# The last phase of an attention and two-layer kernel: element-wise stages of different later steps in one fixed order on each engine, and finished sums copied out by two engines

## The chip, the cores and the metric

The kernel runs on one core of a Trainium2 chip. The core has five engines that work side by side: PE (TensorE, matrix products), DVE (VectorE), ACT (ScalarE), POOL (GpSimd) and SP (SyncE, which here only issues transfers). The metric is the device time of one launch in microseconds (us); lower is better. Before the change it is 1274.14 us (median of three runs, 1273.32 to 1274.87).

## The reference, cut to what matters

```python
# q, k, v: (4, 12, 448, 64);  x between the parts: (1792, 768);  w_in: (768, 2048), w_out: (2048, 768)
q_n, k_n = rmsnorm(q, g_q), rmsnorm(k, g_k)
attn = softmax(q_n @ k_n.T / sqrt(64))
x = (attn @ v), heads put side by side      # 1792 tokens x 768
h = x @ w_in;  g = s * relu(h)**2 + b;  x = g @ w_out      # first layer
h = x @ w_in2; g = h * cos(h);          x = g @ w_out2     # second layer
```

All is float32. The change lies in the second layer: nearly all of it in its last line's second half, `g = h * cos(h)` and `g @ w_out2`.

## The kernel before, in words

Every float32 operand of a product is split in a high part (rounded to the matrix engine's float32 form) and a low part, `hi + lo`, and a product is the sum of three: hi·hi, lo·hi, hi·lo. So each operand costs a cast (ACT) and a subtraction (POOL or DVE).

The second layer has two phases. **Phase one** makes `h` in eight chunks of 256 of the 2048 columns, for two halves `pr` of the tokens (896 tokens each, "0" and "1"). From chunk 2 on for half 0, and from chunk 3 on for half 1, a chunk of one half is seven products of combined operands in place of eight (Strassen's scheme): the combined tokens are the tiles `x_t` (`t1` to `t4`, each in three pieces c), the combined weights `ps`. `mix_tasks` makes the `t` tiles in 21 small tasks; `chunk_tasks` hands such tasks to the steps of the chunk ahead, and `spread_out` spaces each list evenly over that chunk's steps. `h` goes to DRAM (`hd`).

**Phase two** (`second_out`) makes the output. The 14 blocks of 128 tokens are taken in five groups of 3, 3, 3, 3 and 2 (`GROUPS`). A group is 16 steps, one for each 128 of the 2048 rows of `w_out2`; a step multiplies the group's piece of `g` (the tile `gp`: hi and lo) with that weight (`wo_h`, `wo_l`): 18 matmuls with three blocks, 12 with two, into one PSUM bank for each block and half of the output columns. A group of three holds six of the eight banks. When its sixteenth step is done DVE copies each bank out (`o`, line 1209), and SP stores it. The next group has two banks that are free; for the third it needs the first copy.

For every step, piece by piece: SP fetches `h` (`ask`, five steps ahead, tile `g`); then `prepare_g`, three steps ahead, runs the whole chain for that step: `times_cos` (lines 993 to 999), and the split into `gp` (1162 on ACT, 1163 on POOL). The cosine is a chain over three engines:

```python
nc.scalar.activation(kk, h, AF.Copy, scale=1.0 / (2 * math.pi), bias=MAGIC)   # 993 ACT
nc.scalar.activation(kk, kk, AF.Copy, bias=-MAGIC)                            # 994 ACT
nc.vector.scalar_tensor_tensor(gt, kk, -C1, h, ALU.mult, ALU.add)             # 995 DVE
nc.vector.scalar_tensor_tensor(gt, kk, -C2, gt, ALU.mult, ALU.add)            # 996 DVE
nc.scalar.activation(gt, gt, AF.Abs)                                          # 997 ACT
nc.scalar.activation(gt, gt, AF.Sin, scale=-1.0, bias=halfpi)                 # 998 ACT
nc.gpsimd.tensor_tensor(h, h, gt, ALU.mult)                                   # 999 POOL
```

`kk` and `gt` (in the trace `kk` and `ct`) have two buffers each, `g` has six, `gp` has eight. The first group needs no cosine here: phase one has already applied it to its tokens. The 16 weights are split by `prepare_w`, seven steps ahead (`wo_h` on ACT, `wo_l` on DVE and POOL in turn). The order in which the instructions of one engine stand is set by a scheduler that plays the program through at build time with its own costs; matmuls alone are tied to program order (`mm`). An engine works its list strictly in that order, so an instruction that waits holds up all behind it.

Of the kernel before, what the change touches and what calls it, by code (L numbers as in the profile page):

```python
# [43 lines left out]
def body(ctx, tc, q, k, v, g_q, g_k, w1_in, w1_out, s_in, b_in, w2_in, w2_out, out):  # L44
# [1082 lines left out]

    LEADING, ASKED, NEARBY = 3, 5, 7
    STEPS_2 = [(gi, f) for gi in range(len(GROUPS)) for f in range(NF)]
    asked, ready = {}, {}  # L1130

    def columns(gi):
# [7 lines left out]
        return at  # L1140

    def ask(n):
        if n >= len(STEPS_2):
# [8 lines left out]
    def prepare_g(n):  # L1152
        if n >= len(STEPS_2):
            return
        gi, f = STEPS_2[n]
        u = asked.pop(n)
# [268 lines left out]
```

## Time and profile before

| | before |
|---|---|
| median of three runs | 1274.14 us |
| the profiled execution's own time | 1275.54 us |
| its span, first to last instruction | 1273.7 us |
| busy in the span: PE, DVE, ACT, POOL | 1215.9, 865.6, 805.5, 727.7 us |
| phase two: first matmul to last | 998.98 to 1268.22 us |

The profile is one execution. All times below count from the start of its span. "Busy" is the time in which an engine has an instruction in work, also while that instruction waits for a port; "idle before" is the time in which it had none, with the instruction that ended it. Matmuls overlap one another, so their cost is read from start to start, not from their durations. The granted clock of PE is 1.00 at full speed (2.4 GHz) and goes down to half of it (1.2 GHz).

### The profile page before, as it was taken

To read this page: it belongs to the slowest core of one execution; us is meant where nothing else is said; L and a number is where in the kernel's file an instruction comes from. 1 tells how busy PE (TensorE), PEld (TensorE's weight loads), DVE (VectorE), ACT (ScalarE), POOL (GpSimd) and SP (SyncE) were. 2 spreads that over 40 slices of the span, in tenths; PEclk is the share of its full clock that TensorE was granted. 3 is DMA by queue.
4 is the path that set the end of the run, shared out by engine and by line. 5 is a ranking of instruction groups with operands and counts; after the bars stand their busy time and mean duration, and the time that the engine had idled before them with its cause. 6 is when DMAs were issued, how large, how long until landed. Compare 5 with 4: busy or idle time off the path is not lost.

```text
span 1273.7 us, 19551 instructions
## 1 busy us (share of the span) xinstructions
PE 1215.9 (95%) x6476; PEld 1033.9 (81%) x6476; DVE 865.6 (68%) x1364; ACT 805.5 (63%) x1819; POOL 727.7 (57%) x870
## 2 busy tenths in 40 slices
PE   7999999999999999999999999988999997979898
PEld 5555777778778778889899999877899897979898
DVE  6888769766868754865776685798887355555541
ACT  4888888766666654588655664655554566566652
POOL 4776657455363433656766574656645675666542
PEclk8999999999999999999999999989999898989899
DMA  5334335433433326635434354665554733131221
GB/s 142 98 107 117 107 102 174 146 126 109 132 106 116 100 91 197 205 106 168 129 118 138 108 156 160 187 197 168 179 178 165 249 94 93 49 89 56 85 68 45
DMA packets 123446, 164.35 MB, mean 129 GB/s; under 512 B 15824, under 2 KB 111312, under 8 KB 123344
## 3 DMA queue, kind: packets, MB, share of 16 engines
q1 hardware_dynamic: 123184, 163.07, 41.5%
q8 instruction: 51, 0.84, 0.3%
q14 instruction: 51, 0.42, 0.1%
q10 hardware_dynamic: 160, 0.03, 0.0%
HBM read 115.74 MB, written 47.32 MB: 128 GB/s over the span
## 4 chain that ended last, share of the span: by engine, by line
PE 31%; DVE 10%; ACT 6%; DMA 4%; issue 4%; POOL 3%; SPq 0%; DVEq 0%; ACTq 0%; POOLq 0%
PE po L800 10%; PE ph_s L1021 4%; DVE ct L996 4%; PE ph_s L709 3%; DVE ct L995 3%; PE ph_a L1021 3%; PE ph_a L709 3%; PE po L1021 3%; PE ph L1030 2%; PE ph L764 2%; DMA g<-hd 2%; ACT ct L997 1%; ACT kk L994 1%; POOL gp L1163 1%; ACT ct L998 1%
## 5 line engine op out<-in xcount | busy, mean ns | idle before, releaser
L1021 PE MATMUL po<-wo_h,gp 128*128 128x384 f32 x896 | 235.6, 344 | 27.7 <-DVE o L1209 25.0
L1021 PEld LDWEIGHTS po<-wo_h,gp 128*128 128x128 f32 x896 | 167.4, 194 | 30.0 <-DVE o L1209 26.3
L1021 PE MATMUL po<-wo_l,gp 128*128 128x384 f32 x448 | 153.1, 342 | 0.0
L545 POOL TENSOR_TENSOR wl<-t,wh 128x384 fp32r<-128x384 f32 x94 | 98.9, 1066 | 69.7 <-ACT wh L542 60.2
L808 DVE TENSOR_TENSOR acc<-po,acc 128x448 f32<-128x448 f32 (+2 forms) x168 | 101.5, 617 | 53.5 <-PE po L800 52.8
L995 DVE SCALAR_TENSOR_TENSOR ct<-kk,g 128x384 f32<-128x384 f32 (+1 forms) x64 | 47.2, 737 | 97.6 <-ACT kk L994 86.5
L354 ACT ACTIVATE pr<-sc,top 128x448 f32<-128x448 f32 x161 | 102.3, 640 | 16.5 <-DVE top L342 16.0
L342 DVE TENSOR_REDUCE top<-sc 128x1 f32<-128x448 f32 x168 | 98.2, 615 | 17.5 <-PE sc L327 16.7
L1163 POOL TENSOR_TENSOR gp<-g,gp 128x384 fp32r<-128x384 f32 (+1 forms) x80 | 90.4, 1137 | 30.0 <-ACT gp L1162 28.4
L999 POOL TENSOR_TENSOR g<-g,ct 128x384 f32<-128x384 f32 (+1 forms) x64 | 62.0, 970 | 64.1 <-ACT ct L998 64.0
L379 PE MATMUL tp<-ident,pr 128*112 128x128 f32 x672 | 95.2, 278 | 1.1 <-DVE pT L391 0.5
L800 PE MATMUL po<-gh,wh 128*128 128x448 f32 (+1 forms) x240 | 92.1, 386 | 3.8 <-DVE acc L808 3.2
L379 PEld LDWEIGHTS tp<-ident,pr 128*112 128x112 f32 x672 | 74.6, 134 | 24.9 <-issue 13.5
L764 PE MATMUL ph<-xha,wh 128*128 128x448 f32 (+2 forms) x240 | 89.8, 375 | 0.0
L764 PE MATMUL ph<-xla,wh 128*128 128x448 f32 (+2 forms) x240 | 88.3, 368 | 0.0
L764 PE MATMUL ph<-xha,wl 128*128 128x448 f32 (+2 forms) x240 | 88.2, 368 | 0.0
L800 PE MATMUL po<-gh,wl 128*128 128x448 f32 (+1 forms) x240 | 87.8, 366 | 0.0
L800 PE MATMUL po<-gl,wh 128*128 128x448 f32 (+1 forms) x240 | 87.5, 367 | 0.0
L1021 PEld LDWEIGHTS po<-wo_l,gp 128*128 128x128 f32 x448 | 87.0, 194 | 0.0
L997 ACT ACTIVATE ct<-ct 128x384 f32<-128x384 f32 (+1 forms) x80 | 40.1, 502 | 71.2 <-DVE ct L996 71.1
L414 PE MATMUL av<-pT,rawv 112*64 112x448 f32 x384 | 80.0, 546 | 0.7 <-PE rt L398 0.7
L996 DVE SCALAR_TENSOR_TENSOR ct<-kk,ct 128x384 f32<-128x384 f32 (+1 forms) x80 | 78.0, 975 | 2.1
(223 smaller groups left out, 3297.4 us busy)
## 6 DMA issues: line engine op xcount, KB each, us to landing
raw<-in_moe_w_in_dram SPq DMA_DIRECT2D x64, 384.0 KB, 3.6
rawo<-in_moe_w_out_dram SPq DMA_DIRECT2D x32, 384.0 KB, 3.7
wd<-t SPq DMA_DIRECT2D x64, 192.0 KB, 2.6
raw<-in_moe_w_out_dram SPq DMA_DIRECT2D x32, 384.0 KB, 3.3
hd<-u SPq DMA_DIRECT2D x44, 224.0 KB, 2.4
t<-wd SPq DMA_DIRECT2D x48, 192.0 KB, 2.7
g<-hd SPq DMA_DIRECT2D x48, 192.0 KB, 2.4
wo<-to SPq DMA_DIRECT2D x32, 192.0 KB, 2.2
```

What stands on the lines that cost most here:

```text
L342: line("DVE", nc.vector.tensor_reduce(top, st[i]["sc", c][j][1][:, :S], axis=AX.X, op=ALU.max, negate=True))
L354: e = line("ACT", nc.scalar.activation(pr, sc[:, :S], AF.Exp, bias=st[i]["top"][:, at], scale=scale, accum_out=st[i]["sums"][:, at]))
L379: mm = [nc.tensor.transpose(tp[:, kc * P:(kc + 1) * P], pr[:, kc * CP:(kc + 1) * CP], ident) for kc in range(NCH)]
L414: mm.append(nc.tensor.matmul(st[i]["pa"][j * D:(j + 1) * D, :], st[i]["v"][:, j, kc, :], st[i]["pT"][:, j, kc, :], start=(kc == 0), stop=( ...
L545: casts.append((count["needed"], z, eng, eng.tensor_tensor(wl, w, wh.bitcast(F32), ALU.subtract)))
L764: nc.tensor.matmul(h, a, m, start=(c == 0 and n == 0), stop=(c == NE - 1 and n == 2))
L800: marks["out"] = nc.tensor.matmul(po, a, m, start=(f == 0 and n == 0), stop=(f == CF - 1 and n == 2))
L808: marks["DVE"] = nc.vector.tensor_tensor(at, po, at, ALU.add)
L995: nc.vector.scalar_tensor_tensor(gt, kk, -C1, h, ALU.mult, ALU.add)
L996: nc.vector.scalar_tensor_tensor(gt, kk, -C2, gt, ALU.mult, ALU.add)
L1021: z = nc.tensor.matmul(*args, **kw)
L1163: nc.gpsimd.tensor_tensor(lo, u, f32(hi), ALU.subtract)
```

## The change

1. `prepare_g` falls apart into stages. After the matmuls of step n, the program issues: split of step n+2 (`halve_g`), multiplication for n+3 (`times_g`), Abs and Sin for n+4 (`turned_g`), the two DVE operations for n+5 (`residue`), rounding for n+6 (`rounded`), and the fetch for n+8 (`ask`).
2. `in_line` ties these instructions, the weights' split and the copies to program order, one chain for each of ACT, DVE and POOL.
3. The tiles come from nine large tiles of phase one that are no longer needed (`spare`): eight buffers for `g`, four for `kk`, five for `ct`.
4. The bank copies of a group follow the sixteenth step's stages: one half of the output columns on DVE, the other on ACT. The last block's two halves are stored apart, by SP and by the ACT queue.
5. `wo_l` is made by DVE alone. Before phase two three pieces are asked for and two split, where it was five and three.
6. In phase one the 21 mixing tasks get ten empty ones behind them, so they fall in the first two thirds of their chunk.

```diff
@@ chunk_tasks
-                lists.append([z for c in range(half) for z in mix_tasks(pr, c)])
+                mixing = [z for c in range(half) for z in mix_tasks(pr, c)]
+                lists.append(mixing + [lambda: None] * (len(mixing) // 2))
...
-            lists.append([lambda: None] * 14 + [lambda z=z: ask(z) for z in range(ASKED)] + [lambda z=z: prepare_g(z) for z in range(LEADING)])
+            lists.append([lambda: None] * 12 + [lambda z=z: (ask(z), z < HI and halve_g(z)) for z in range(HI + 1)])
...
-    LEADING, ASKED, NEARBY = 3, 5, 7
+    NEARBY = 7
+    HI, TIMES, TURNED, RESIDUE, ROUNDED, ASKED = 2, 3, 4, 5, 6, 8
...
+    def in_line(eng, z):
+        if eng in chains:
+            issue_after(z, chains[eng])
+        chains[eng] = z
+
+    def temp(n, kind):
+        size = len(GROUPS[STEPS_2[n][0]]) * P
+        at, many = {"g": (0, 8), "kk": (8, 4), "ct": (12, 5)}[kind]
+        at += n % many
+        return spare[at // 2][:, at % 2 * S:at % 2 * S + size]
...
+    def rounded(n):
+        if STEPS_2[n][0]:
+            kk = work[n, "kk"] = temp(n, "kk")
+            in_line("ACT", nc.scalar.activation(kk, work[n, "g"], AF.Copy, scale=1.0 / (2 * math.pi), bias=MAGIC))
+            in_line("ACT", nc.scalar.activation(kk, kk, AF.Copy, bias=-MAGIC))
...
+    def residue(n):
+        if STEPS_2[n][0]:
+            kk, ct = work.pop((n, "kk")), temp(n, "ct")
+            work[n, "ct"] = ct
+            in_line("DVE", nc.vector.scalar_tensor_tensor(ct, kk, -C1, work[n, "g"], ALU.mult, ALU.add))
+            in_line("DVE", nc.vector.scalar_tensor_tensor(ct, kk, -C2, ct, ALU.mult, ALU.add))
...
+    def halve_g(n):
+        u = work.pop((n, "g"))
...
+        in_line("ACT", nc.scalar.copy(hi, u))
+        in_line("POOL", nc.gpsimd.tensor_tensor(lo, u, f32(hi), ALU.subtract))
...
-        (nc.vector if f % 2 else nc.gpsimd).tensor_tensor(lo, t, f32(hi), ALU.subtract)
+        in_line("ACT", nc.scalar.copy(hi, t))
+        in_line("DVE", nc.vector.tensor_tensor(lo, t, f32(hi), ALU.subtract))
...
@@ second_out, after the matmuls of step n
-                if f == NF - 1:
-                    o = wp.tile([P, E], F32, tag="wh", name=f"o_{t}", bufs=3)
-                    for eh in range(2):
-                        nc.vector.tensor_copy(o[:, eh * EH:(eh + 1) * EH], po[t, eh])
-                    store(t, o)
+            if n == 0:
+                for z in range(2 * NF, 2 * NF + 9):
+                    spare.append(f32(slot(homes[z - 2 * NEARBY], f"sp_{z}")))
+            if n:
+                halve_g(n + HI)
+            times_g(n + TIMES)
+            turned_g(n + TURNED)
+            residue(n + RESIDUE)
+            rounded(n + ROUNDED)
+            for z in range(HI + 1 if n == 0 else n + ASKED, n + ASKED + 1):
+                ask(z)
+            if n == 0:
+                halve_g(HI)
             if n + NEARBY < NF:
                 prepare_w(n + NEARBY)
-            ask(n + ASKED)
-            prepare_g(n + LEADING)
+            if f < NF - 1:
+                continue
+            for t in GROUPS[gi]:
+                o = wp.tile([P, E], F32, tag="wh", name=f"o_{t}", bufs=3)
+                for eh in range(2):
+                    es = slice(eh * EH, (eh + 1) * EH)
+                    if eh:
+                        in_line("ACT", nc.scalar.copy(o[:, es], po[t, eh]))
+                    else:
+                        in_line("DVE", nc.vector.tensor_copy(o[:, es], po[t, eh]))
+                    if t == 2 * NT - 1:
+                        store(t, o, es, (nc.sync, nc.scalar)[eh])
+                if t < 2 * NT - 1:
+                    store(t, o, slice(0, E), nc.sync)
```

What stands on DVE where the first group ends, before. In `ct_2_26` the 26 is the step; steps 0 to 15 are the first group, and `o_0` to `o_2` are its three blocks:

```order
L995 SCALAR_TENSOR_TENSOR ct_2_25_12155<-kk_2_25_12154,g2_25_12088 128x384
L996 SCALAR_TENSOR_TENSOR ct_2_25_12155<-kk_2_25_12154,ct_2_25_12155 128x384
L995 SCALAR_TENSOR_TENSOR ct_2_26_12187<-kk_2_26_12186,g2_26_12120 128x384
L996 SCALAR_TENSOR_TENSOR ct_2_26_12187<-kk_2_26_12186,ct_2_26_12187 128x384
L1209 COPY o_0_11898<-po2_0_0_0_11469 128x384
L1209 COPY o_0_11898<-po2_0_0_1_11470 128x384
L1209 COPY o_1_11908<-po2_0_1_0_11471 128x384
```

And now (the two halves of `sp_38` hold `ct` of step 20, above the copies, and of step 21, below them; `sp_36` holds `kk`, `sp_34` `g`):

```order
L1181 SCALAR_TENSOR_TENSOR sp_38_11492<-sp_36_11490,sp_34_11488 128x384
L1182 SCALAR_TENSOR_TENSOR sp_38_11492<-sp_36_11490,sp_38_11492 128x384
L1271 COPY o_0_11921<-po2_0_0_0_11462 128x384
L1271 COPY o_1_11925<-po2_0_1_0_11464 128x384
L1271 COPY o_2_11929<-po2_0_2_0_11466 128x384
L1181 SCALAR_TENSOR_TENSOR sp_38_11492<-sp_36_11490,sp_34_11488 128x384
L1182 SCALAR_TENSOR_TENSOR sp_38_11492<-sp_36_11490,sp_38_11492 128x384
```

The copies stood behind the work for step 26 and now stand behind that for step 20; there are three of them in place of six.

What stands on ACT there now (`gp_17` and `gp_18` are the high parts of steps 17 and 18, L1188 and L1189 Abs and Sin, L1173 and L1174 the rounding):

```order
L1203 CAST gp_17_11910<-sp_32_11486 128x384
L1188 ACTIVATE sp_40_11494<-sp_40_11494 128x384
L1189 ACTIVATE sp_40_11494<-sp_40_11494,halfpi_81 128x384
L1173 ACTIVATE sp_36_11490<-sp_34_11488 128x384
L1174 ACTIVATE sp_36_11490<-sp_36_11490 128x384
L1269 COPY o_0_11921<-po2_0_0_1_11463 128x384
L1269 COPY o_1_11925<-po2_0_1_1_11465 128x384
L1269 COPY o_2_11929<-po2_0_2_1_11467 128x384
L1203 CAST gp_18_11957<-sp_33_11487 128x384
```

The other three copies stand on ACT, ahead of the split of step 18.

What stands on POOL in phase one, before chunk 2 (`x1_0_t2_2` is piece 2 of the combined tokens t2 of half 0, `ps` and `pa` are chunk 2's weights), before:

```order
L943 TENSOR_TENSOR ps2_2_9624<-s2_2_9622,ps2_2_9624 128x384
L943 TENSOR_TENSOR ps3_2_9658<-pl_2_1_9525,ps3_2_9658 128x384
L943 TENSOR_TENSOR ps1_2_9661<-s1_2_9591,ps1_2_9661 128x384
L943 TENSOR_TENSOR pa12_2_9701<-pl_2_0_9433,pa12_2_9701 128x384
L869 TENSOR_TENSOR x1_0_t1_2_9673<-xs_0_2_x11_9665,x1_0_t1_2_9673 128x448
L554 TENSOR_SCALAR c_o_21_9712<-c_o_21_9712 128x384
L943 TENSOR_TENSOR pa22_2_9741<-pl_2_1_9525,pa22_2_9741 128x384
L943 TENSOR_TENSOR ps4_2_9746<-s4_2_9744,ps4_2_9746 128x384
L869 TENSOR_TENSOR x1_0_t2_2_9675<-xs_0_2_x22_9669,x1_0_t2_2_9675 128x448
```

And now:

```order
L869 TENSOR_TENSOR x1_0_t1_2_9613<-xs_0_2_x11_9605,x1_0_t1_2_9613 128x448
L943 TENSOR_TENSOR ps2_2_9645<-s2_2_9643,ps2_2_9645 128x384
L943 TENSOR_TENSOR ps3_2_9680<-pl_2_1_9540,ps3_2_9680 128x384
L943 TENSOR_TENSOR ps1_2_9683<-s1_2_9600,ps1_2_9683 128x384
L869 TENSOR_TENSOR x1_0_t2_2_9615<-xs_0_2_x22_9609,x1_0_t2_2_9615 128x448
L943 TENSOR_TENSOR pa12_2_9712<-pl_2_0_9433,pa12_2_9712 128x384
L554 TENSOR_SCALAR c_o_21_9718<-c_o_21_9718 128x384
L943 TENSOR_TENSOR pa22_2_9747<-pl_2_1_9540,pa22_2_9747 128x384
L943 TENSOR_TENSOR ps4_2_9752<-s4_2_9750,ps4_2_9752 128x384
```

Piece 2 of t2 stands ahead of four instructions that it stood behind; three of these are low parts of weights, and `t1` (piece 2) now stands ahead of the first weight.

What SP has to issue near the end of phase one, before (`g2_0` and `g2_1` are steps 0 and 1, `tw` the weights, `u` parts of `h` on their way out):

```order
L1149 DMA g2_1_11370<-hd_1_0_9180 128x384
L1007 DMA hd_14_0_11276<-u2_7_0_11226 128x448
L1174 DMA tw_6_11459<-wo_6_8014 128x768
L1174 DMA tw_7_11495<-wo_7_8242 128x768
L1007 DMA hd_14_0_11276<-u1_7_0_11214 128x448
L1007 DMA hd_15_0_11263<-u3_7_0_11238 128x448
L1149 DMA g2_0_11368<-hd_0_0_9010 128x384
```

And now:

```order
L1166 DMA g2_0_11414<-hd_0_0_9010 128x384
L1215 DMA tw_6_11456<-wo_6_8014 128x768
L1007 DMA hd_14_0_11276<-u2_7_0_11226 128x448
L1166 DMA g2_1_11437<-hd_1_0_9180 128x384
L1215 DMA tw_7_11506<-wo_7_8242 128x768
L1166 DMA sp_32_11486<-hd_8_0_10475 128x384
L1166 DMA sp_32_11486<-hd_9_0_10451 128x384
L1007 DMA hd_14_0_11276<-u1_7_0_11214 128x448
```

The fetch for step 0 stands ahead of two weights and three stores of `h` that it stood behind; the fetches for steps 8 and 9 stand here too, and that for step 2 (not shown) comes 18 places after step 0's, behind the fetches of steps 3 to 10 and five stores.

## Rows read from the trace of the kernel before

**Rows 1.** Waits in phase two: waiter, releaser, us in total, times, longest

```profile
PE po L1021 <- DVE o L1209: 25.0, 4, 9.0
```

**Rows 2.** Timeline of PE, phase two: start, us, instruction, count [idle before <-releaser]

```profile
998.98 0.69 PE L1021 MATMUL po<-wo_h,gp 128*128 128x384 f32 x1 [2.31 <-ACT gp L1162]
...
1050.12 0.51 PE L1021 MATMUL po<-wo_h,gp 128*128 128x384 f32 x2
...
1050.63 0.51 PE L1021 MATMUL po<-wo_h,gp 128*128 128x384 f32 x2
...
1062.70 1.01 PE L1021 MATMUL po<-wo_h,gp 128*128 128x384 f32 x2 [8.79 <-DVE o L1209]
...
1123.95 1.01 PE L1021 MATMUL po<-wo_h,gp 128*128 128x384 f32 x2 [9.01 <-DVE o L1209]
...
1235.70 0.62 PE L1021 MATMUL po<-wo_h,gp 128*128 128x384 f32 x2 [1.30 <-DVE o L1209]
...
1267.88 0.34 PE L1021 MATMUL po<-wo_l,gp 128*128 128x384 f32 x1
```

**Rows 3.** Stretches: length; PE, PEld, DVE, ACT, POOL busy (count); clock, DMA, GB/s

```profile
850.00:860.00 10.00, 10.00 (x51) 9.28 (x50) 9.98 (x14) 6.13 (x12) 5.46 (x5) 1.00 0.67 199
...
1000.00:1010.00 10.00, 9.94 (x42) 9.94 (x43) 2.18 (x2) 3.42 (x5) 5.07 (x5) 0.71 0.95 316
...
1040.00:1050.00 10.00, 10.00 (x60) 10.00 (x59) 5.61 (x7) 6.64 (x15) 6.48 (x6) 1.00 0.22 61
...
1060.00:1070.00 10.00, 7.29 (x30) 7.30 (x31) 8.36 (x12) 4.86 (x11) 5.94 (x6) 0.64 0.50 173
```

**Rows 4.** Timeline of DVE around the end of the first group

```profile
1052.59 1.01 DVE L995 SCALAR_TENSOR_TENSOR ct<-kk,g 128x384 f32<-128x384 f32 x1 [2.04 <-ACT kk L994]
1053.63 1.24 DVE L996 SCALAR_TENSOR_TENSOR ct<-kk,ct 128x384 f32<-128x384 f32 x1
1055.99 0.56 DVE L995 SCALAR_TENSOR_TENSOR ct<-kk,g 128x384 f32<-128x384 f32 x1 [1.12 <-ACT kk L994]
...
1059.92 0.99 DVE L995 SCALAR_TENSOR_TENSOR ct<-kk,g 128x384 f32<-128x384 f32 x1 [2.04 <-ACT kk L994]
...
1062.11 1.47 DVE L1209 COPY o<-po 128x384 f32<-128x384 f32 x3
```

**Rows 5.** Timeline of POOL, same place, and its first two splits

```profile
999.01 1.96 POOL L1163 TENSOR_TENSOR gp<-g,gp 128x384 fp32r<-128x384 f32 x2 [2.28 <-ACT gp L1162]
...
1052.16 1.02 POOL L999 TENSOR_TENSOR g<-g,ct 128x384 f32<-128x384 f32 x1 [0.74 <-ACT ct L998]
1053.14 1.32 POOL L1163 TENSOR_TENSOR gp<-g,gp 128x384 fp32r<-128x384 f32 x1
```

**Rows 6.** Timeline of ACT: five in a row near 1052, and the first splits

```profile
998.42 0.93 ACT L1162 CAST gp<-g 128x384 fp32r<-128x384 f32 x2 [2.22 <-DMA g<-hd]
...
1050.64 0.53 ACT L997 ACTIVATE ct<-ct 128x384 f32<-128x384 f32 x1 [1.20 <-DVE ct L996]
...
1052.40 0.50 ACT L1162 CAST gp<-g 128x384 fp32r<-128x384 f32 x1
```

**Rows 7.** POOL's groups of 256 columns, the last group's two operations

```profile
L999 POOL TENSOR_TENSOR g<-g,ct 128x256 f32<-128x256 f32 x16 | 12.3, 766 | 2.9 <-ACT ct L998 2.8
L1163 POOL TENSOR_TENSOR gp<-g,gp 128x256 fp32r<-128x256 f32 x16 | 11.7, 738 | 16.2 <-ACT gp L1162 16.2
```

**Rows 8.** Timeline of PE, phase one, chunk 2's half 0 and the start of chunk 3

```profile
824.44 2.02 PE L1021 MATMUL ph_a<-x_b,pa 128*128 128x448 f32 x9
...
830.09 0.68 PE L1021 MATMUL ph_s<-x_t,ps 128*128 128x448 f32 x2 [2.39 <-ACT x_t L874]
834.10 6.12 PE L1021 MATMUL ph_s<-x_t,ps 128*128 128x448 f32 x19 [3.33 <-POOL x_t L869]
...
845.52 14.75 PE L1021 MATMUL ph<-x_b,pa 128*128 128x448 f32 x72
...
863.08 5.64 PE L1021 MATMUL ph_s<-x_t,ps 128*128 128x448 f32 x26 [0.77 <-POOL ps L943]
```

More of the change, by code (lines that the diff above doesn't have):

```diff
@@ L1126, in second_in @@
                     todo.pop(0)[1]()
-    LEADING, ASKED, NEARBY = 3, 5, 7
+    NEARBY = 7
+    HI, TIMES, TURNED, RESIDUE, ROUNDED, ASKED = 2, 3, 4, 5, 6, 8
     STEPS_2 = [(gi, f) for gi in range(len(GROUPS)) for f in range(NF)]
-    asked, ready = {}, {}
+    work, ready = {}, {}
+    spare = []
+    chains = {}
+    def in_line(eng, z):
[7 more added lines that the diff above has]
+        return spare[at // 2][:, at % 2 * S:at % 2 * S + size]
     def columns(gi):
@@ L1140, in columns, with staged @@
         return at
+    def staged(f):
+        return lambda n: n < len(STEPS_2) and f(n)
+    @staged
     def ask(n):
-        if n >= len(STEPS_2):
-            return
         gi, f = STEPS_2[n]
-        u = asked[n] = u_tile(f"g2_{n}")[:, :len(GROUPS[gi]) * P]
+        u = work[n, "g"] = temp(n, "g") if spare else u_tile(f"g2_{n}")[:, :len(GROUPS[gi]) * P]
         at = 0
@@ L1150, in ask, with turned_g, times_g @@
             at += size
[L1152 to L1156, printed above, removed]
+    @staged
+    def rounded(n):
[3 more added lines that the diff above has]
+            in_line("ACT", nc.scalar.activation(kk, kk, AF.Copy, bias=-MAGIC))
+    @staged
+    def residue(n):
[4 more added lines that the diff above has]
+            in_line("DVE", nc.vector.scalar_tensor_tensor(ct, kk, -C2, ct, ALU.mult, ALU.add))
+    @staged
+    def turned_g(n):
+        if STEPS_2[n][0]:
+            ct = work[n, "ct"]
+            in_line("ACT", nc.scalar.activation(ct, ct, AF.Abs))
+            in_line("ACT", nc.scalar.activation(ct, ct, AF.Sin, scale=-1.0, bias=halfpi))
+    @staged
+    def times_g(n):
+        if STEPS_2[n][0]:
+            u = work[n, "g"]
+            in_line("POOL", nc.gpsimd.tensor_tensor(u, u, work.pop((n, "ct")), ALU.mult))
+    @staged
+    def halve_g(n):
+        u = work.pop((n, "g"))
         size = u.shape[1]
-        if gi:
-            times_cos(u, f"2_{n}")
         t = part(f"gp_{n}")
         hi, lo = ready[n] = t[:, :size], t[:, CW:CW + size]
-        nc.scalar.copy(hi, u)
-        nc.gpsimd.tensor_tensor(lo, u, f32(hi), ALU.subtract)
+        in_line("ACT", nc.scalar.copy(hi, u))
+        in_line("POOL", nc.gpsimd.tensor_tensor(lo, u, f32(hi), ALU.subtract))
     homes = []
@@ L1174, in prepare_w, with store @@
         nc.sync.dma_start(t, wd[f])
-        nc.scalar.copy(hi, t)
-        (nc.vector if f % 2 else nc.gpsimd).tensor_tensor(lo, t, f32(hi), ALU.subtract)
+        in_line("ACT", nc.scalar.copy(hi, t))
+        in_line("DVE", nc.vector.tensor_tensor(lo, t, f32(hi), ALU.subtract))
         W["out", f] = hi, lo
-    def store(t, o):
+    def store(t, o, cols, queue):
         pr, j0 = t // NT, t % NT * P
@@ L1186, in store @@
                 n = min(P - p, j0 + P - j)
-                rows = out[b * S:b * S + CUT, :].rearrange("(p c) e -> c p e", c=NW)[c, p:p + n, :]
+                rows = out[b * S:b * S + CUT, :].rearrange("(p c) e -> c p e", c=NW)[c, p:p + n, cols]
             else:
                 n = min(S - n0, j0 + P - j)
-                rows = out[b * S + n0:b * S + n0 + n, :]
-            nc.sync.dma_start(rows, o[j - j0:j - j0 + n, :])
+                rows = out[b * S + n0:b * S + n0 + n, cols]
+            queue.dma_start(rows, o[j - j0:j - j0 + n, cols])
             j += n
```

## The prediction

> **What bounds the kernel now.** I read the busy times first: PE is at work for 95% of the span, so time can only come from gaps in PE and from matmuls at a lower clock. I then read the waits of phase two, and PE's timeline there. One wait stands out: PE for DVE's copies of finished sums, 25.0 us in four times [rows 1]. The timeline places them at the ends of the first four groups: 8.79, 9.01 and 1.30 us [rows 2], and 5.9 for the one not shown there, from the sum; a stop of 2.31 us precedes the first matmul. At full speed three matmuls take 0.52 us from start to start [rows 2], so a step of 18 takes 3.12. Phase two has 64 x 18 + 16 x 12 = 1344 matmuls, 233 us of work, and lasts from 998.98 to 1268.22, 269.2 us [rows 2]. Of the 36 us between, 25.0 are the four stops; 11.2 remain. The stretches explain most of these: after the first stop the granted clock is 0.64, and 30 matmuls take 7.29 us in place of 5.2, 2.1 lost; in 1000 to 1010 it is 0.71, and 42 take 9.94 in place of 7.3, 2.6 lost [rows 3]. The stop of 1.30 us is followed by nearly full speed. So three long stops cost 6.3 us of clock, the start 2.6, and about 2 are scattered.
>
> Why is DVE late with the copies? In 1040 to 1050 no engine but PE is full: DVE 5.61, ACT 6.64, POOL 6.48 of 10 us [rows 3]. DVE waits for ACT's rounding every time, and two steps take it 1059.92 - 1052.59 = 7.33 us, 3.67 a step [rows 4]. That is a chain of seven dependent operations with two buffers, not a lack of throughput. DVE's list has the first copy behind step 26, so its lag against PE, 0.55 x 16 = 8.8 us a group, becomes the stop.
>
> **The change part by part.** *Stages.* Five ACT instructions take 2.26 us in a row (1050.64 to 1052.40 + 0.50) [rows 6]. POOL's two take 0.98 each in a row (1.96 for two), DVE's 0.56 each where nothing disturbs them [rows 4, 5]. So a step needs 2.3, 2.0 and 1.1 us, each under 3.12. Stages of different steps wait only for what was done an iteration earlier, with one exception: POOL's multiplication, ACT's split, POOL's subtraction and the next multiplication follow each other. A handover costs 0.09: the first split ends at 998.92, and POOL starts at 999.01 [rows 5, 6]. This loop takes 1.02 + 0.09 + 0.50 + 0.09 + 0.98 = 2.7 us.
>
> DVE lengthens it. Its L995 at 1052.59 took 1.01 us because POOL's L999 was at work until 1053.18, and the same instruction at 1055.99 took 0.56; POOL's subtraction at 1053.14 took 1.32 and not 0.98, and L996 at 1053.63 took 1.24 beside that [rows 4, 5]. They take turns: the four instructions of a step need 1.96 + 1.12 = 3.08 us together, 0.04 under PE's 3.12. The loop leaves POOL free for 0.7 us, which holds one DVE instruction; the second adds from nothing to 0.56. The pace is 2.7 to 3.2, and I take 3.0, since the second can start in the same gap.
>
> The Trainium skill, "SBUF — State Buffer", section "Who interferes with whom", says that a DVE instruction with two SBUF inputs and a GpSimd instruction that reads SBUF exclude each other for the whole instruction, and that whoever issues first holds the port. The rows agree: the three long durations above are each a wait for the other's end plus the undisturbed time. By this rule the pace is 3.0 where DVE finds POOL's gap and 3.8 where it comes first every time, which is the slower rival below.
>
> *Copies.* They stand on DVE behind step 20 now, and three of six on ACT. At 3.0 a step both engines get there before PE has finished the group. PE needs the third bank 1.04 us after its last matmul (six matmuls go into free banks); that copy can start as soon as the first block is done, 2 us earlier, and takes 0.49 (1.47 for three) [rows 4]. ACT's copies cost about as much as its cast, 0.50 [rows 6]. I keep 0.4 us a boundary; the bounds are 0 and 9.01. ACT then resumes with the split of the group's third step: 0.6 + 0.5 + 0.1 + 1.0 = 2.2 us after the end, where PE needs it 6.2 after. This lead of 4 us covers a pace up to 3.12 + 4 / 16 = 3.37. Gain at the boundaries: 25.0 - 1.6 + 6.3 = 29.7 us.
>
> *The last group* has 12 matmuls, 2.08 us a step. Its loop is 0.77 + 0.74 [rows 7], two handovers and a split (0.4, scaled from 0.50): 2.1. DVE's part may add 0.3, which the lead pays. Cost nothing; without the lead, 5.
>
> *Start.* Step 0's fetch stands five places earlier on SP, so ACT's wait for it (2.22 us) [rows 6] goes, and with it the stop of 2.31 and the 2.6 us of clock. Late next is step 2: its fetch stands behind eight others and five stores, in a stretch where the transfers run at 316 GB/s [rows 3]. From the moment the stores' data are there (estimate: 996, the end of phase one), three stores of 229 KB, a weight of 393 and, itself included, five fetches of 197 have to pass, 2.06 MB or 6.5 us, so split and subtraction end near 1004; PE would be there at 1002.9. I take a stop of 1.3 us without loss of clock, as at 1235.70. Gain 3.6; bounds 4.9 and -3.
>
> *Free of cost.* Weights' subtractions all on DVE: it is busy 2.18 of 10 us in 1000 to 1010 [rows 3]; were it late, the splits behind the weights' casts on ACT would be late too, but each stands four steps ahead of its need. More buffers remove ACT's waits for fetches, which were not on PE's path. The last block's halves leave on two engines: one copy less at the end, 0.4 (0 to 0.5).
>
> *Mixing.* Chunk 2's half 0 takes 845.52 - 824.44 = 21.1 us; its seven products at the later rate (72 matmuls in 14.75 us, 1.82 for nine) need 12.8 [rows 8]. 8.3 are lost to two waits for piece 2 of t2, 2.39 and 3.33, and to the clock after them. That piece now stands four POOL instructions earlier, some 5 us. But DVE is full there, 9.98 of 10 [rows 3], and in its new list three mixing instructions stand ahead of chunk 3's first combined weight, for which PE waits already (0.77) [rows 8]. Most of what PE gains it meets again there. Bounds +7 and -4; I take 2.
>
> *Sum.* 29.7 + 3.6 + 0.4 + 2 = 35.7 us. The profiled execution took 1275.54 (span 1273.7), which gives 1239.8; the median of the runs is 1.4 lower, so 1238.
>
> **The rivals.** *Taking turns costs more.* For it: 0.04 us of reserve a step, and three of the four instructions disturbed at 1052.59 to 1054.9 [rows 4, 5]. Against: a lead of 4 us per group, and fewer buffers' waits. At 3.5 a step 48 steps lose 0.38 x 48 = 18 us, less 4 of lead in each of three groups, 6, and the last group 4: 1248. It decides from 3.37.
>
> *Mixing returns with a loss.* For it: DVE is full in 850 to 860 [rows 3]. It would give -4 in place of +2, 1244.
>
> *The start stops again.* For it: the fetch for step 2. A stop over 2 us costs the clock too: 2.31 + 2.6 + 2 in place of 1.3, 1244.
>
> *Slower.* Both DVE instructions of a step get the port ahead of POOL's two, each time: the loop is 2.7 + 1.1 = 3.8, more than the 3.67 of now. 48 steps lose 0.68 x 48 = 33 us, the last group 0.8 x 16 = 13, less 4: 42 us, 1280. It decides from about 3.7. The port rule of the Trainium skill named above allows this, as the first comer holds the port. Against: POOL would have to lose every race, and POOL's gap comes just when DVE can use it.
>
> **How the numbers follow.** Forecast 0.52, turns 0.18, mixing 0.14, start 0.13, slower 0.03. The predicted time is the first's, 1238. Its own range is 1230 to 1244. The range of 8 in 10 takes in the three rivals that stay faster, and below the +7 of mixing and the scattered 2 us: 1228 to 1252. Under 0.2% (2.5 us) a measurement of this kernel can't tell a difference from none. Faster needs only that more than a tenth of the 35.7 arrives: 0.96; within 0.2%: 0.01; slower: 0.03.
>
> **What would show it.** In PE's timeline the three stops of 6 to 9 us at the group ends must be gone, with under 1 us each left, and the granted clock be 1.00 throughout phase two; it should last 235 to 240 us from first to last matmul. DVE's L1181 should come every 3.1 us, held up by PE and no longer by ACT. Step 0 should start within 0.5 us of phase one's end; a stop before step 2 or 3, released by POOL's subtraction, is the start's term. Chunk 2's half 0 should take 13 to 16 us, and chunk 3 start with a longer wait than 0.77. I am wrong if PE still waits for copies over 2 us a group, if POOL's subtraction is what PE waits for in the middle of a group, or if the loss of chunk 2 is found whole in chunk 3.

## The result, and the profile after

| | before | after |
|---|---|---|
| median (lowest to highest), four runs each | 1274.09 us (1273.32 to 1274.87) | 1241.43 us (1241.07 to 1243.94) |
| span of the profiled execution | 1273.7 us | 1239.9 us |
| phase two, first matmul to last | 269.2 us | 242.1 us |
| busy: PE, DVE, ACT, POOL | 1215.9, 865.6, 805.5, 727.7 us | 1204.9, 829.9, 820.6, 715.9 us |

The ratio is 0.9748, 95% interval 0.9731 to 0.9765. The forecast was 1238, its range 1228 to 1252.

The wait that stood out before, PE for the copies [rows 1], is gone; now the copying engines wait for PE. These are the waits of phase two (waiter, releaser, us in total, times, longest):

```profile
DVE o L1271 <- PE po L1021: 34.7, 14, 9.6
ACT o L1269 <- PE po L1021: 26.4, 14, 8.5
...
ACT gp L1203 <- DMA g<-hd: 12.0, 2, 11.6
```

PE's timeline (start, us, instruction, count, idle before and releaser) shows all stops of phase two. They are in its first 14 us; none lies at a group's end, where [rows 2] had four. The second group begins at 1051.78:

```profile
992.89 0.51 PE L1021 MATMUL po<-wo_h,gp 128*128 128x384 f32 x2
...
996.79 0.62 PE L1021 MATMUL po<-wo_h,gp 128*128 128x384 f32 x2 [1.64 <-DVE u L1058]
...
1004.95 0.69 PE L1021 MATMUL po<-wo_h,gp 128*128 128x384 f32 x1 [3.72 <-ACT gp L1203]
1006.03 0.69 PE L1021 MATMUL po<-wo_h,gp 128*128 128x384 f32 x1 [0.39 <-POOL gp L1204]
...
1051.78 0.51 PE L1021 MATMUL po<-wo_h,gp 128*128 128x384 f32 x2
...
1234.64 0.34 PE L1021 MATMUL po<-wo_l,gp 128*128 128x384 f32 x1
```

The stretches, columns as in [rows 3]. The clock of 0.64 in 1060 to 1070 has become 1.00; the 0.71 behind the start is still there. In 1040 to 1050 the other engines rest, because they have reached the copies and wait for PE:

```profile
850.00:860.00 10.00, 4.25 (x21) 3.58 (x20) 10.00 (x16) 5.64 (x12) 5.54 (x6) 0.85 0.82 246
860.00:870.00 10.00, 8.19 (x27) 6.98 (x28) 10.00 (x9) 5.92 (x13) 10.00 (x8) 0.64 0.33 119
1000.00:1010.00 10.00, 5.90 (x21) 5.18 (x20) 2.78 (x2) 2.81 (x5) 4.20 (x3) 0.69 0.53 179
1040.00:1050.00 10.00, 10.00 (x59) 10.00 (x59) 0.56 (x1) 1.42 (x4) 1.61 (x2) 1.00 0.07 21
...
1060.00:1070.00 10.00, 10.00 (x60) 10.00 (x59) 4.29 (x8) 8.62 (x18) 7.50 (x8) 1.00 0.25 73
```

DVE's timeline, the place of [rows 4]. It waits 9.61 us for the first bank; later L1181 comes every 2.86 us:

```profile
1049.38 0.56 DVE L1271 COPY o<-po 128x384 f32<-128x384 f32 x1 [9.61 <-PE po L1021]
...
1060.55 0.59 DVE L1181 SCALAR_TENSOR_TENSOR sp<-sp,sp 128x384 f32<-128x384 f32 x1 [1.67 <-ACT sp L1174]
1061.18 0.56 DVE L1182 SCALAR_TENSOR_TENSOR sp<-sp,sp 128x384 f32<-128x384 f32 x1
1063.41 0.59 DVE L1181 SCALAR_TENSOR_TENSOR sp<-sp,sp 128x384 f32<-128x384 f32 x1 [1.67 <-ACT sp L1174]
```

POOL there. The gap of 0.62 us is the predicted loop, multiplication, split on ACT, subtraction; DVE's first instruction fits into it, and the subtraction takes 1.26 in place of 0.98 [rows 5] beside DVE's second:

```profile
1058.49 1.26 POOL L1204 TENSOR_TENSOR gp<-sp,gp 128x384 fp32r<-128x384 f32 x1 [0.62 <-ACT gp L1203]
1059.71 1.01 POOL L1195 TENSOR_TENSOR sp<-sp,sp 128x384 f32<-128x384 f32 x1
1061.35 1.26 POOL L1204 TENSOR_TENSOR gp<-sp,gp 128x384 fp32r<-128x384 f32 x1 [0.62 <-ACT gp L1203]
1062.57 1.01 POOL L1195 TENSOR_TENSOR sp<-sp,sp 128x384 f32<-128x384 f32 x1
```

The fetch of step 2 on SP, between the last store of `h` that stands ahead of it and the split on ACT that waits for it:

```profile
998.14 0.38 SPq L1007 DMA_DIRECT2D hd<-u  x1
...
999.24 0.32 SPq L1166 DMA_DIRECT2D g<-hd  x1
```

```profile
1004.39 0.51 ACT L1203 CAST gp<-g 128x384 fp32r<-128x384 f32 x1 [11.60 <-DMA g<-hd]
```

PE in phase one, against [rows 8]. Chunk 2's half 0 now takes 837.66 - 823.44 = 14.2 us (before 21.1), and chunk 3's half 0 875.71 - 852.25 = 23.5 (before 15.5, from 860.12 to 875.57), with a stop of 6.59 us where it had one of 0.77:

```profile
823.44 2.02 PE L1021 MATMUL ph_a<-x_b,pa 128*128 128x448 f32 x9
...
837.66 14.75 PE L1021 MATMUL ph<-x_b,pa 128*128 128x448 f32 x72
852.25 1.99 PE L1021 MATMUL ph_a<-x_b,pa 128*128 128x448 f32 x9
860.84 0.74 PE L1021 MATMUL ph_s<-x_t,ps 128*128 128x448 f32 x1 [6.59 <-ACT ps L942]
...
875.71 2.02 PE L1021 MATMUL ph_a<-x_b,pa 128*128 128x448 f32 x9
...
901.75 2.02 PE L1021 MATMUL ph_a<-x_b,pa 128*128 128x448 f32 x9
```

The same places before:

```profile
860.12 1.99 PE L1021 MATMUL ph_a<-x_b,pa 128*128 128x448 f32 x9
...
875.57 1.99 PE L1021 MATMUL ph_a<-x_b,pa 128*128 128x448 f32 x9
...
905.38 2.02 PE L1021 MATMUL ph_a<-x_b,pa 128*128 128x448 f32 x9
```

The matmuls behind them, up to the last line of each, take 901.75 - 875.71 = 26.0 us now and 29.8 before, so much of chunk 3's loss comes back there.

### The profile page after: what moved, and what is told of

Read it like the earlier page. It is cut to its first block, busy times and chain, and to the rows that moved or that the text cites. A ratio compares the mean times of both kernels' runs of the same rounds, so it can differ in the third digit from the quotient of the medians.

```text
span 1239.9 us, 19524 instructions
## 1 busy us (share of the span) xinstructions
PE 1204.9 (97%) x6476; PEld 1026.3 (83%) x6476; DVE 829.9 (67%) x1358; ACT 820.6 (66%) x1833; POOL 715.9 (58%) x862
## 4 chain that ended last, share of the span: by engine, by line
PE 49%; DVE 4%; DMA 2%; issue 1%; ACT 1%; POOL 1%; SPq 0%; ACTq 0%; DVEq 0%; POOLq 0%
PE po L1021 18%; PE po L800 10%; PE ph_s L1021 5%; PE ph_a L1021 4%; PE ph_s L709 4%; PE ph_a L709 3%; PE ph L1030 2%; PE ph L764 2%; DVE xs_x L878 1%; DMA hd<-u 1%; DMA xs_x<-yd 1%; DVE x_t L869 0%; DMA g<-hd 0%; DVE u L1058 0%; PE ph L1021 0%
## 5 line engine op out<-in xcount | busy, mean ns | idle before, releaser
L1021 PE MATMUL po<-wo_h,gp 128*128 128x384 f32 x896 | 229.6, 337 | 5.7 <-ACT gp L1203 3.7
L1021 PEld LDWEIGHTS po<-wo_h,gp 128*128 128x128 f32 x896 | 163.0, 189 | 6.9 <-ACT gp L1203 4.0
L1021 PE MATMUL po<-wo_l,gp 128*128 128x384 f32 x448 | 150.6, 336 | 0.0
L1204 POOL TENSOR_TENSOR gp<-sp,gp 128x384 fp32r<-128x384 f32 (+1 forms) x77 | 89.9, 1170 | 75.6 <-ACT gp L1203 73.8
L342 DVE TENSOR_REDUCE top<-sc 128x1 f32<-128x448 f32 x168 | 98.1, 614 | 15.5 <-PE sc L327 14.7
L1181 DVE SCALAR_TENSOR_TENSOR sp<-sp,sp 128x384 f32<-128x384 f32 (+1 forms) x64 | 37.4, 584 | 88.0 <-ACT sp L1174 75.0
L542 ACT CAST wh<-t 128x384 fp32r<-128x384 f32 x112 | 53.3, 510 | 34.6 <-PE po L800 19.8
L774 POOL TENSOR_TENSOR gl<-gt,gh 128x448 fp32r<-128x448 f32 (+2 forms) x40 | 48.0, 1202 | 47.3 <-ACT gh L773 44.5
L1021 PE MATMUL ph_s<-x_t,ps 128*128 128x448 f32 x297 | 66.1, 379 | 8.6 <-ACT ps L942 6.6
```

The source lines that it names most:

```text
L342: line("DVE", nc.vector.tensor_reduce(top, st[i]["sc", c][j][1][:, :S], axis=AX.X, op=ALU.max, negate=True))
L542: z = nc.scalar.copy(wh, w)
L1021: z = nc.tensor.matmul(*args, **kw)
L1204: in_line("POOL", nc.gpsimd.tensor_tensor(lo, u, f32(hi), ALU.subtract))
```

## The experiments

Times are medians; each ratio is to runs of the kernel before on the same chip.

**e1: the kernel before, with only the copies moved in DVE's list.**

```diff
-        nc.vector.scalar_tensor_tensor(gt, kk, -C1, h, ALU.mult, ALU.add)
+        z = nc.vector.scalar_tensor_tensor(gt, kk, -C1, h, ALU.mult, ALU.add)
+        if name.startswith("2_") and last_copy:
+            issue_after(z, last_copy[-1])
...
-                        nc.vector.tensor_copy(o[:, eh * EH:(eh + 1) * EH], po[t, eh])
+                        last_copy.append(nc.vector.tensor_copy(o[:, eh * EH:(eh + 1) * EH], po[t, eh]))
```

> The kernel before, with one edit: DVE's residue of a step whose chain is issued after a group's copies stands behind these copies (steps 18 and on for the first group), as in the kernel after. Chains, buffers and leads stay. Theory A (the stops were a lag of a slow chain, 3.67 us a step against PE's 3.12, paid at the end of a group; the copies' place only says where it is paid): the three stops of 6 to 9 us go, but PE then waits in the middle of each group for the split of the next steps, 0.55 x 14 = 7.7 us a group for three groups, by many short waits on ACT or POOL: 1268 to 1280, about 1274. Theory B (the copies' place in DVE's list alone made the stops): 25 us of idle time and 6 of clock go, 1243 to 1250.

1249.6 us, ratio 0.9809 (0.9789 to 0.983): B, not A. The copies now stand behind step 17 in place of 26. DVE's timeline: it waits 19.60 us for PE, copies all six banks, and the work behind them runs at 5.62 us for two steps (1063.29 to 1068.91), so 2.81 a step. The scheduler has paired the steps:

```profile
1049.89 3.16 DVE L1212 COPY o<-po 128x384 f32<-128x384 f32 x6 [19.60 <-PE po L1023]
1052.97 1.02 DVE L995 SCALAR_TENSOR_TENSOR ct<-kk,g 128x384 f32<-128x384 f32 x2
...
1063.29 0.56 DVE L995 SCALAR_TENSOR_TENSOR ct<-kk,g 128x384 f32<-128x384 f32 x1 [0.90 <-POOL g L1001]
...
1068.91 0.56 DVE L995 SCALAR_TENSOR_TENSOR ct<-kk,g 128x384 f32<-128x384 f32 x1 [0.91 <-POOL g L1001]
```

PE pays one stop of 1.15 us in each of three groups, for the first step behind the copies, and 1.19 in the last:

```profile
1060.14 0.45 PE L1023 MATMUL po<-wo_h,gp 128*128 128x384 f32 x1 [1.15 <-POOL gp L1166]
```

So the old chain was not slow of necessity; it was slow in the order that it had. The edit also changed ACT's order, so "the place alone" includes what the scheduler made of it: the run does not tell the copies' place from the faster pace. What the stages add to it at the boundaries is small: the four stops, 4.6 us together, and some 2 us of slow clock behind them.

**e7: the kernel after without the fixed order.**

```diff
-        if eng in chains:
-            issue_after(z, chains[eng])
         chains[eng] = z
```

> The kernel after, with the stages in the same program order but without the chains that tie ACT, DVE and POOL to it; the scheduler sets the order, and keeps the copies behind the residue of step 20 on DVE, while on POOL two multiplications often stand in a row. Theory A (stages and the copies' place do it, the exact order does not matter): 1240 to 1244. Theory B (the fixed order does it): the leads are used up, PE waits for splits, 1246 to 1260.

1270.6 us, ratio 0.9971 (0.9955 to 0.9986): nearly everything is lost, B and more. The expectation was wrong on one fact: the scheduler puts the copies behind the thirteenth residue, that of step 28, not of 20. And its order on ACT runs Abs, rounding, Sin, rounding, so that DVE waits for ACT and ACT for DVE within the same turn:

```profile
1085.13 1.06 DVE L1179 SCALAR_TENSOR_TENSOR sp<-sp,sp 128x384 f32<-128x384 f32 x1 [1.99 <-ACT sp L1172]
```

```profile
1087.52 0.53 ACT L1186 ACTIVATE sp<-sp 128x384 f32<-128x384 f32 x1 [2.08 <-DVE sp L1180]
1087.95 0.51 ACT L1171 ACTIVATE sp<-sp 128x384 f32<-128x384 f32 x1
1088.37 0.60 ACT L1187 ACTIVATE sp<-sp,halfpi 128x384 f32<-128x384 f32 x1
1088.87 0.51 ACT L1172 ACTIVATE sp<-sp 128x384 f32<-128x384 f32 x1
```

Eight steps from 1077.76 to 1108.57 take 3.85 us each, and PE stops as before:

```profile
1118.72 1.01 PE L1021 MATMUL po<-wo_h,gp 128*128 128x384 f32 x2 [8.75 <-DVE o L1269]
```

Here the stages in program order are worth little unless the engines' lists keep that order. The run lost two things at once, the copies' place and the order of the stages on the engines; how the loss divides between them is not shown.

**e2: all six copies on DVE**, in the same place.

```diff
-                        in_line("ACT", nc.scalar.copy(o[:, es], po[t, eh]))
+                        in_line("DVE", nc.vector.tensor_copy(o[:, es], po[t, eh]))
```

> The kernel after, with all six copies of a group on DVE, in the same place of its list. Theory A (stages bring DVE to the copies early; it waits 9.6 us there for PE): the third bank is still free in time, a copy takes 0.56 us and PE needs one each 0.52, so PE loses under 0.5 us a boundary: 1241 to 1243. Theory B (two engines are what removed the stops): six copies take 3.4 us in a row and hold DVE's residue, PE stops again by 1 to 3 us a boundary with loss of clock: 1248 to 1258.

1240.05 us, ratio 0.9732 (0.9707 to 0.9758): A. DVE waits 7.35 us for the first bank, and the copies follow each other every 0.52 us, PE's own pace for a bank. No stop at any boundary. The second engine isn't needed for this.

```profile
1048.03 0.56 DVE L1271 COPY o<-po 128x384 f32<-128x384 f32 x1 [7.35 <-PE po L1021]
1048.55 0.56 DVE L1269 COPY o<-po 128x384 f32<-128x384 f32 x1
```

**e6: two buffers each for `kk` and `ct`.**

```diff
-        at, many = {"g": (0, 8), "kk": (8, 4), "ct": (12, 5)}[kind]
+        at, many = {"g": (0, 8), "kk": (8, 2), "ct": (12, 2)}[kind]
```

> The kernel after, with two buffers each for kk and ct, as before, in place of four and five. Theory A (the stages alone make the pace; the residue of step n+5 now waits for the multiplication of n+3 in the same turn, which still leaves over 1.5 us): pace 2.9 to 3.1 us a step, 1241 to 1244. Theory B (without spare buffers each step waits for the one two ahead, as before): pace 3.3 to 3.7, 48 steps lose 9 to 28 us less 12 of lead: 1246 to 1262.

1241.78 us, ratio 0.9739 (0.9723 to 0.9755): A. The pace is 3.04 us (1071.76 to 1077.83 for two steps), still under PE's 3.12. The eight buffers of `g` and the longer lead of its fetches stayed; no run takes them back.

```profile
1071.76 0.56 DVE L1181 SCALAR_TENSOR_TENSOR sp<-sp,sp 128x384 f32<-128x384 f32 x1 [1.89 <-POOL sp L1195]
...
1077.83 0.56 DVE L1181 SCALAR_TENSOR_TENSOR sp<-sp,sp 128x384 f32<-128x384 f32 x1 [1.88 <-POOL sp L1195]
```

**e4 and e8: one and two more DVE instructions in each step.** They add zero times `kk`, so the result stays the same.

```diff
             in_line("DVE", nc.vector.scalar_tensor_tensor(ct, kk, -C2, ct, ALU.mult, ALU.add))
+            in_line("DVE", nc.vector.scalar_tensor_tensor(ct, kk, 0.0, ct, ALU.mult, ALU.add))
```

> The kernel after, with a third DVE instruction of the residue's kind in each step of the later groups (it adds zero times kk, so it changes nothing of the result). Theory A (DVE's instructions with two SBUF inputs and POOL's take turns; four of them set the pace of 2.86 us a step): the pace becomes 2.86 + 0.56 = 3.4, over PE's 3.12; 48 steps lose 0.3 x 48 = 14 us, less the leads of about 4 us in each of three groups, and the last group 0.5 x 16 = 8 less 4: 1244 to 1256. Theory B (DVE has room: its two instructions are at work 1.2 to 2 us of a step): nothing changes, 1240 to 1243.

> The kernel after with two more DVE instructions of the residue's kind in each step of the later groups (they add zero times kk). With one, the pace went from 2.86 to 3.18 us a step, and PE had a single stop of 1.14 us. Theory A (DVE and POOL take turns, a lead of about 4 us a group covers paces up to 3.37): each instruction beside POOL's costs 0.3 to 0.6, the pace is 3.5 to 3.8, beyond the cover: 48 steps lose 18 to 33 us, less 12 of lead, the last group 6 to 12 less 4, and clock behind the stops: 1252 to 1275. Theory B (the cover is wider than that, or DVE has room): 1241 to 1246.

One: 1242.97 us, ratio 0.9758 (0.9739 to 0.9778), against 0.9748 for the kernel after. The pace became 3.18 us, not 3.4; that is over 3.12, but the lead covers it but for one stop of 1.14 us at a group's end. A was right on the mechanism and overpriced it. DVE's timeline with one more:

```profile
1058.23 0.92 DVE L1181 SCALAR_TENSOR_TENSOR sp<-sp,sp 128x384 f32<-128x384 f32 x1 [0.38 <-ACT sp L1174]
...
1061.41 0.91 DVE L1181 SCALAR_TENSOR_TENSOR sp<-sp,sp 128x384 f32<-128x384 f32 x1 [0.37 <-ACT sp L1174]
```

Two: 1273.84 us, ratio 0.9995 (0.9984 to 1.0006), the whole gain lost, as A said. In 1070 to 1080 DVE is at work for 9.76 of 10 us. PE stops in the middle of a group every second step, 1105.49 - 1097.98 = 7.51 us apart, so 3.75 a step, and then for the copies at the group's end:

```profile
1097.98 0.44 PE L1021 MATMUL po<-wo_h,gp 128*128 128x384 f32 x1 [0.90 <-POOL gp L1206]
1105.49 0.44 PE L1021 MATMUL po<-wo_h,gp 128*128 128x384 f32 x1 [0.89 <-POOL gp L1206]
1112.57 1.01 PE L1021 MATMUL po<-wo_h,gp 128*128 128x384 f32 x2 [5.94 <-DVE o L1273]
```

**e5: edit 6 undone**, the empty tasks left out of the mixing list.

```diff
-                lists.append(mixing + [lambda: None] * (len(mixing) // 2))
+                lists.append(mixing)
```

> The kernel after, without edit 6 (no empty tasks behind the mixing tasks). Theory A (as predicted: chunk 2 gains 7 us and chunk 3 loses most of it): 1 to 4 us slower than the kernel after, 1242 to 1245; phase one ends 1 to 4 us later than the 991.9 to 993.1 of the runs with the edit. Theory B (everything is given back; the profiles' earlier end of phase one is scatter from run to run): within 1 us, 1240 to 1242.

1241.29 us, ratio 0.9742 (0.9727 to 0.9757): the same as with it, B; by the two intervals the edit is worth 0 within 3 us. Phase one ends at 990.42 here; in the traces of kernels with the edit at 989.99 (e8) to 993.05 (e4), in those without at 990.42 to 996.67 (the kernel before). An earlier end of phase one in a single trace says nothing. Nor does the part where the edit works: from the start of chunk 2's half 0 to the matmul that is shown above at 901.75 (905.38 before), the eight traces with the edit take 77.4 (e6) to 79.5 us (e4), the four without it 77.5 (e5) to 80.9 (the kernel before).

**e3 and e10: the start.** e3 takes the spare tiles from slots that come free at the middle of phase one's last chunk, and fetches steps 0 to 2 into them as well; e10 also splits the weights five steps ahead in place of seven.

```diff
     def ask(n):
+        if not spare:
+            for z in range(9):
+                spare.append(f32(slot(kept[z], f"sp_{z}")))
...
+            kept.extend(homes[2 * NEARBY:2 * NEARBY + 9])
+            del homes[2 * NEARBY:2 * NEARBY + 9]
...
-    NEARBY = 7
+    NEARBY = 5        # e10 alone
```

> The kernel after, with the nine spare tiles taken from slots that come free at the middle of phase one's last chunk (the weights of steps 7 to 15 take the later ones), and steps 0 to 2 fetched into them too, not into tiles of h. Theory A (the two stops at the start, 1.64 us for a bank held by DVE's sum that waits for a store of h, and 3.72 + 0.39 for the fetch of step 2, come from the place of that fetch on SP and from its tile): both go or stay under 1 us together, no half clock after them: 5 to 8 us less, 1233 to 1237. Theory B (the transfers at the end of phase one are the bound, 304 to 399 GB/s from 990 to 1010): what is fetched early delays stores of h and weights by as much; the stops move, 1239 to 1243.

> The kernel of e3 with the weights split five steps ahead in place of seven, so that two fetches of 393 KB and two splits leave the end of phase one. Theory A (what is left of the start, three stops of 0.6 to 1.8 us behind DVE's sums of phase one, comes from DVE's list, where these sums stand behind weights' subtractions that wait for fetches): one or two of the stops go, 2 to 4 us less than e3, 1234 to 1236. Theory B (the sums wait for their own buffers and POOL): as e3, 1237 to 1239; or the weights are late in the first group, 1240.

e3: 1237.98 us, ratio 0.972 (0.9697 to 0.9743), between A and B; the interval overlaps that of the kernel after. In the trace the stop for step 2's fetch is gone, and in 1000 to 1010 the clock is 0.87 in place of 0.69; but three stops behind DVE's sums of phase one remain, 3.2 us together, so A in part. (The 304 to 399 GB/s of the expectation are not what the trace of the kernel after shows: 289 in 990 to 1000, 179 in 1000 to 1010.) e10: 1234.53 us, ratio 0.9682 (0.9653 to 0.971), one stop left:

```profile
996.58 0.62 PE L1021 MATMUL po<-wo_h,gp 128*128 128x384 f32 x2 [1.91 <-DVE u L1058]
```

The interval does not touch that of the kernel after (0.9731 to 0.9765), so the start's cost is shown; it overlaps that of e3. That DVE's list held the sums is what e10 suggests; it took two fetches away as well, and which of the two it was stays open.

**e9, e11, e12: the start with variants of edit 6.** e9 is e3 without edit 6, e11 is e3 with it for half 0 alone, e12 is e10 with it for half 0 alone.

```diff
-                lists.append(mixing + [lambda: None] * (len(mixing) // 2))
+                lists.append(mixing + [lambda: None] * (0 if pr else len(mixing) // 2))
```

> The kernel of e3 (spare tiles that come free early, steps 0 to 2 fetched into them) without edit 6. The two are far apart in time (840 to 880 and 990 to 1010 us), so their effects add: e3 was 3.5 us faster than the kernel after, e5 the same as it. 1236 to 1239. If edit 6 has a cost that shows only where the start no longer hides it (theory B: phase one ends earlier without it, 990.4 against 991.9 to 993.1), 1234 to 1236.

> The kernel of e3 with edit 6 for half 0 alone (the mixing tasks of half 1, in chunk 2, spread over the whole chunk again). Theory A (chunk 3's late weight comes from DVE being full in 840 to 870, with the mixing tasks of half 1 crowded there): chunk 2 keeps its gain of some 7 us and chunk 3 loses less than 8: 1232 to 1237. Theory B (DVE has the same work to do before chunk 3 and less time for it, since chunk 2 ends earlier): given back as before, 1236 to 1240.

> The kernel of e10 (spare tiles free early, weights five steps ahead) with edit 6 for half 0 alone, as in e11. If both effects are real and add up: e10 lay 3 to 4 us below e3, e11 up to 3 us: 1229 to 1233. If e11's difference from e3 is scatter (their intervals overlap): as e10, 1233 to 1236.

e9 1239.41 us, ratio 0.9726 (0.9699 to 0.9754), just above the 1236 to 1239 expected; e11 1235.28, 0.9685 (0.9656 to 0.9713); e12 1231.13, 0.9661 (0.9646 to 0.9675), in the range for two effects that add up. But e9 and e11 overlap e3, e12 overlaps e10, so edit 6 for one half is not shown to help. In the traces e12 ends phase one no earlier than e10 (992.87 against 991.89); what it has ahead of e10 lies in phase two. And the stops in chunk 3 are 4.05 and 3.72 us in e11, no less in sum than 6.08 and 0.98 in e3. e12 as a whole beats both kernels, and its interval lies apart from that of the kernel after. Its phase two has no stop at all and takes 992.87 to 1226.01, 233.1 us, the 233 that its matmuls cost; its first stretches:

```profile
990.00:1000.00 10.00, 10.00 (x57) 9.74 (x56) 6.08 (x9) 3.74 (x6) 4.14 (x3) 1.00 0.90 284
1000.00:1010.00 10.00, 10.00 (x59) 10.00 (x59) 3.72 (x4) 4.99 (x8) 4.52 (x4) 1.00 0.74 230
```

## Why the prediction was right, and where not

By the two traces (spans 1273.7 and 1239.9, 33.8 us less):

| term | predicted | measured |
|---|---|---|
| boundaries | 29.7 | 32.3 |
| start | 3.6 | -2.9 |
| tail | 0.4 | 0.6 |
| mixing, phase one | 2 | 3.8 in these traces, 0 within 3 by e5 |

The boundaries are measured from the second group's first matmul to the last of all, at 1267.88 before [rows 2]. The first one in the kernel before:

```profile
1052.71 0.51 PE L1021 MATMUL po<-wo_h,gp 128*128 128x384 f32 x2
```

That is 215.2 us before and 1234.64 - 1051.78 = 182.9 now, about what the 1056 matmuls cost at 0.52 for three. The 32.3 us hold the 25.0 of the stops, so the clock behind them had cost 7.3 and not the 6.3 of the prediction. The start is the stretch from phase one's end (996.67 before, 992.89 now) to the second group's first matmul: 56.0 us before, 58.9 now.

*Boundaries: right in size, half right in cause.* The stops came from copies that stood behind eleven steps' work; that step held. But the prediction called the lag, 0.55 us a step, the chain's own, and used 3.67 as its pace. That pace belonged to the old order. With the same buffers and the same instructions e1 shows 2.81, and its time falls by 24 us, where the whole change gives 32.7. In the kernel before DVE came to the first residue of the second group at 1027.33, here in its timeline:

```profile
1027.33 1.29 DVE L995 SCALAR_TENSOR_TENSOR ct<-kk,g 128x384 f32<-128x384 f32 x1
```

The copies stood behind eleven of them, the last at 1059.92 [rows 4], so 3.26 us each; two of them in place of eleven, in the order that followed from it, were enough.

*Pace: right.* 2.86 was measured, 3.0 taken, 2.7 to 3.2 the bounds, by the loop and the gap that were named. One reading under it is off: the disturbed instructions of [rows 4] and [rows 5] do not take "the other's end plus the undisturbed time". L995 ended at 1053.60, 0.42 us after L999 (1053.18), where it takes 0.56 undisturbed; POOL's subtraction ended at 1054.46, 0.86 after L995, where it takes 0.98. So the 3.08 us for four instructions were too many (last section). The cover up to 3.37 is not contradicted: 3.18 cost one stop of 1.14 us and nothing that the times can tell, 3.75 cost 32 us (e4, e8); where between the two it ends is not shown. The slower rival was priced at 1280 for 3.8 (1268, had it taken off the lead in each group, as the rival of turns does); e8 gave 1273.8 at 3.75. It did not come: POOL has the gap in every step shown.

*Handover at the copies: too careful.* 0.4 us a boundary was kept, 0 was measured, by ACT and DVE waiting for PE, or by DVE alone (e2).

*Start: wrong, the rival "the start stops again" came true.* Step 0 starts without a stop, as predicted. But step 2's fetch left SP only at 999.24, its split began at 1004.39, and PE stood 3.72 and 0.39 us, not 1.3; the clock behind it (0.69 in 1000 to 1010) was lost as well. The step that failed is "from the moment the stores' data are there (estimate: 996, the end of phase one)": phase one ended at 992.89, but the last of the three stores ahead of the fetch left SP at 998.14, 5 us later, and the fetch behind it. So split and subtraction ended near 1006 (PE waits for them up to 1006.03) and not 1004, and PE was there earlier, at 1001.23 and not 1002.9. The transfers were priced by bytes alone; when the fetch may go, by SP's list and by its tile, was the other part (e3 changed both, so which of them holds it is not shown). The rival's own price, 2.31 + 2.6 + 2 in place of 1.3, is 5.6 us; the start came out 6.5 us below the forecast. The stop of 1.64 us for a bank that a DVE sum still held was not foreseen; before, PE began phase two only at 998.98 [rows 2] and shows no such stop.

*Mixing: the direction named, the rest not shown.* Of "most of what PE gains it meets again" the first chunk behind shows all: 6.9 us gained in chunk 2's half 0 and 8.0 lost in chunk 3's, which the prediction had named as a sign of being wrong. DVE has no idle time in 850 to 870, as it had next to none before. What it did not see is that 3.8 us come back right behind (29.8 to 26.0). The sum of the three, 2.6 us in these two traces, is within the scatter of the others (e5).

*Costless edits.* More buffers for `kk` and `ct` (e6) and the second copying engine (e2) gained nothing that can be measured, as costed. The weights' subtractions on DVE alone and the buffers of `g` were in every run with the stages; they were not tested.

*Signs.* Three of those named did not come: the clock was 0.69 behind the start, phase two took 242.1 us and not 235 to 240, and L1181 came every 2.86 us, held up by ACT (1.67); PE held DVE up only at the copies. The first two are the start's.

The predicted sum came close in part by luck: a boundary term 2.6 too small made up for some of a start term 6.5 too large, and 1.8 more came from phase one, which is no more than its scatter between traces. e1, whose edit touches phase two alone, ended it 3.3 us earlier than the kernel before, at 993.35.

## What to carry to other kernels

An engine's stop at a hand-over is a question about lists: count what stands ahead of the instruction that frees the buffer, and when each of these can run. Moving the copies forward, with the order that followed from it, was worth 24 us here, while more buffers for `kk` and `ct` and a second copying engine were worth nothing that could be measured. A pace that is read from a trace belongs to the order in that trace; before it is used as a limit, add up the loop that really depends on itself. And part of the gain of a staged program is in the engines' lists: without the fixed order, which also moved the copies back, the same stages gave back some 28 of 33 us.

## What the runs showed of the hardware that was not expected

DVE's and POOL's instructions take turns, but for less than their recorded time. One step of the kernel after shows it, in the lines of DVE and POOL above. POOL's multiplication ends at 1060.72; DVE's first instruction, begun before that, ends at 1061.14, 0.42 us later; DVE's second ends at 1061.74, 0.60 later; POOL's subtraction, begun before that, ends at 1062.61, 0.87 later; the next multiplication ends at 1063.58, 0.97 later. Together these are the 2.86 us of the pace. The instruction that had to wait needs 0.42 (DVE) or 0.87 (POOL) behind the other's end, where it takes 0.56 and 0.98 undisturbed. The recorded times of the four add up to 3.1, and of five and six to 3.7 and 4.2, but the paces were 2.86, 3.18 and 3.75. Read in the same way, the steps of e4 (from 1058.72 to 1061.90) and e8 (two of them, from 1091.71 to 1099.22) are filled too, but for hundredths of a microsecond: one of the two engines has an instruction in work, and the waiting one ends 0.41 to 0.43 (DVE) or 0.85 to 0.88 (POOL) after the other.

The Trainium skill, "SBUF — State Buffer", section "Who interferes with whom", says that a DVE instruction with two SBUF inputs contends with a GpSimd instruction that reads SBUF, and calls the contention on their shared ports an exclusive lock. The trace agrees that each waits for the other, as the subtraction of 1.26 us shows, but the recorded duration is not the time that is held: about 0.1 us of it, by the 0.42 and 0.87 above, passes beside the other's.
